# A one-element VectorE write ahead of GpSimd's first sum over the keys, in a band attention fused with a feed-forward layer

## The chip, the cores and the metric

The kernel runs on one core of one Trainium2 chip. The metric is the device time of one execution in microseconds (us); the time of a kernel is the median over its runs. Engines are named as the profile names them: PE is TensorE with its matmuls, PEld its weight loads, DVE is VectorE, ACT is ScalarE, POOL is GpSimd and SP is SyncE.

## The reference, cut to what matters

Attention over 8 batches of 8 heads, 576 positions and head size 64, in which each position sees itself and the 63 before it. Its output, as 4608 tokens of 512 numbers, goes through a feed-forward layer with 2048 hidden units.

```python
scores = scale * np.matmul(q, k.transpose(0, 1, 3, 2))
rel = pos[:, None] - pos[None, :]
scores = np.where((rel >= 0) & (rel < 64), scores, -1e9)
scores = scores - np.max(scores, axis=-1, keepdims=True)
attn = np.exp(scores)
attn = attn / (np.sum(attn, axis=-1, keepdims=True) + 1e-09)
x = np.matmul(attn, v).transpose(0, 2, 1, 3).reshape(4608, 512)
h = x @ w_in
out = np.maximum(0.01 * h, h) @ w_out
```

## The kernel before

**Attention.** The 576 positions of a batch are cut into nine blocks of 64 queries; each block of queries sees 128 keys. That makes 72 units, and two neighbouring units make a pair m. A pair's scores lie with the 128 keys on the partitions, in two halves j of 128x512 numbers. Maximum and sum over the keys are therefore taken across partitions, and POOL does both, with `partition_all_reduce`.

**Feed-forward.** The tokens are cut into nine chunks of 512, and the hidden units into sixteen blocks f of 128. One job (c, f) is 12 matmuls in `mm1` (line 539), which make 128 hidden units of 512 tokens, and 12 in `mm2` (line 586), which add their part of the output. Each product of two float32 tensors is made of three products of rounded parts: high by high, high by low, low by high. So after `mm1` ACT applies the leaky maximum (line 544, tile `g`) and rounds the result (line 550, tile `gh`), and then DVE subtracts to get the low part (line 554, tile `gl`). Four times in `mm2`, once for each 128 tokens, two matmuls with `gh` as weights are followed by one with `gl`. Tile `g` has one buffer, `gh` and `gl` have two each.

**The last stage.** The loop at the end of `band_attention_ffn` (from `open_room()` on) runs the jobs of chunks 2 to 8. Pairs 12 to 35 are worked in between them, two at a time: a group is eight jobs, numbered `at` from 0 to 7, with the pairs m (even, probabilities in tile `e`) and m + 1 (odd, in tile `late_e`). There are twelve groups; the last sixteen jobs have none. Below, "job 2 of a group" is the job with `at == 2`. Within a group:

- Job 1: after `mm1` and the `mm2` of job 0, PE makes the scores of both pairs (line 239); DVE scales and masks them (line 477); POOL takes the four maxima (line 486); DVE subtracts the maxima of pair m (line 492) and ACT takes the exponential (line 493). Then the `mm2` of job 1 is put in at once, so that the `mm1` of job 2 and of job 3 stand one behind the other on PE, followed by the `mm2` of job 2.
- Job 2: `mm1` with its leaky maximum, rounding and low part; then `exps_3(m + 1)`, the two subtractions of DVE and the two exponentials of ACT for the second pair; then three sums of POOL (line 497): pair m with j = 0 into slot 0 of tile `late_n`, pair m with j = 1 into the spare tile (`n` in the profile, tag `pT`), pair m + 1 with j = 0 into slot 1 of `late_n`.
- Job 4: `fold_3(m)` on DVE: two additions (lines 501 and 502) that bring the two halves' sums together, and a reciprocal (line 503). Then POOL's fourth sum, pair m + 1 with j = 1, into the spare tile that `fold_3(m)` has just read.
- Job 5: PE multiplies the probabilities of both pairs with the values (line 512); DVE does `product_3(m)`, `fold_3(m + 1)` and `low_3(m)`.
- Job 6: DVE does `product_3(m + 1)` and `low_3(m + 1)`.

The spare tile has one buffer. It holds the last maximum (pair m + 1, j = 1) until DVE has subtracted it, then the second sum, then the fourth. Slot 0 of `late_n` holds the maximum of pair m with j = 1 before it takes the first sum; slot 1 holds that of pair m + 1 with j = 0 before it takes the third.

**What sets the order.** The order on each engine is the order in which the program issues the instructions; a loop at the end of the function ties every instruction to the one before it on its engine. Between engines the framework adds waits from what each instruction reads and writes.

Of the kernel before, what the change touches and what calls it, by code (L numbers as in the profile page):

```python
# [88 lines left out]
def band_attention_ffn(ctx: ExitStack, tc: tile.TileContext, qT, kB, vW, vL, w_in, w_out, eye_mask, out):  # L89
    nc = tc.nc  # L90
# [49 lines left out]
    def load_q(m):  # L140
        if m < NU // 2:
            nc.sync.dma_start(q_of(m), qT[m])

    def load_k(m):
        if m < NU // 2:
            nc.sync.dma_start(k_of(m), kB[m])

    def load_v(m):
        if m < NU // 2:
            nc.sync.dma_start(v_of(m), vL[m - PAIRED] if m >= PAIRED else vW[m])  # L150
# [302 lines left out]
    later = {}  # L453
# [8 lines left out]
    def e_of(m):  # L462
        return (probs_of, later["e"])[m % 2]

    def scores_3(m):
        ps = [bank(t, f"s{m}_{j}") for j, t in enumerate((next(of_h), next(of_h)) if m % 2 else "st")]
        quarter_scores(m, ps, False)
        probs[m] = ps

    def shield_3(m):  # L470
        ps = probs.pop(m)
        a = mask_of(UNITS * m).bitcast(F32)
        n = a.shape[1]
        a = flat(a)[:, None, :].broadcast_to([P, H // n, n * QB])
        for j in range(2):
            e, s = (x.rearrange("a (b c) -> a b c", c=n * QB) for x in (e_of(m)[:, j], ps[j]))
            nc.vector.scalar_tensor_tensor(e, s, SCALE, a, ALU.mult, ALU.add)  # L477

    def spare(name):
        return wk.tile([P, 512], F32, tag="pT", bufs=1, name=name)  # L480

    def most_3(m):
        for j in range(2):
            b = 2 * (m % 2) + j
            mx = later["n"][:, b - 1] if b in (1, 2) else spare(f"mx{m}_{j}")
            nc.gpsimd.partition_all_reduce(mx, e_of(m)[:, j], P, ReduceOp.max)  # L486
            probs[m, j] = mx

    def exps_3(m):
        for j in range(2):  # L490
            e = e_of(m)[:, j]
            nc.vector.tensor_tensor(e, e, probs.pop((m, j)), ALU.subtract)  # L492
            nc.scalar.activation(e, e, AF.Exp)  # L493

    def sums_3(m, j):
        t = probs[m, "sum"] = spare(f"n{m}") if j else later["n"][:, m % 2]
        nc.gpsimd.partition_all_reduce(t, e_of(m)[:, j], P, ReduceOp.add)  # L497

    def fold_3(m):
        r, t = later["n"][:, m % 2], probs.pop((m, "sum"))  # L500
        nc.vector.tensor_scalar_add(r[64:], t[64:], 1e-9)  # L501
        nc.vector.tensor_scalar_add(r[:64], r[:64], 1e-9)
        nc.vector.reciprocal(r, r)  # L503

    def values_3(m):
        ps = bank("st"[m % 2], f"o{m}")
        for w in range(UNITS):
            v = v_heads(m, w)
            for p in range(NP):
                for j in range(2):  # L510
                    c = (2 * p + w) * QB
                    nc.tensor.matmul(  # L512
                        ps[64 * j : 64 * j + 64, c : c + QB], v[:, 2 * p + j], e_of(m)[:, j, c : c + QB],
                        start=True, stop=True,
                    )
        probs[m] = ps

    def product_3(m):
        r = later["n"][:, m % 2]
        nc.vector.tensor_tensor(r, probs.pop(m), r, ALU.mult)  # L520
        nc.scalar.copy(x_of(UNITS * m)[0], r.rearrange("a (b c) -> a b c", b=NP))

    def low_3(m):
        hi, lo = x_of(UNITS * m)
        t = later["n"][:, m % 2].rearrange("a (b c) -> a b c", b=NP)
        nc.vector.tensor_tensor(lo, t, hi.bitcast(F32), ALU.subtract)
# [5 lines left out]
    def mm1(c, f, part):  # L532

        xh, xl = xs[c]
        ps = bank(next(of_h) if c or f >= half else "h", f"h{c}_{f}_{part.start}")[:, part]
        wh, wl = wi[f]
        terms = [(a, b, k) for k in range(KT) for a, b in ((wh, xh), (wh, xl), (wl, xh))]
        for n, (a, b, k) in enumerate(terms):
            nc.tensor.matmul(ps, a[:, k, :], b[:, k, part], start=n == 0, stop=n == len(terms) - 1)  # L539
        t = []  # L540

        def leak():
            t.append(wk.tile([P, CH], F32, tag="g", bufs=1, name=f"g{c}_{f}_{part.start}")[:, part])
            nc.scalar.activation(t[0], ps, AF.Prelu, alpha=0.01)  # L544

        def high():
            g[c, f, part.start] = [
                wk.tile([P, CH], F32R, tag=n, name=f"{n}{c}_{f}_{part.start}") for n in ("gh", "gl")
            ]
            nc.scalar.copy(g[c, f, part.start][0][:, part], t[0])  # L550

        def low():
            hi, lo = (x[:, part] for x in g[c, f, part.start])
            nc.vector.tensor_tensor(lo, t[0], hi.bitcast(F32), ALU.subtract)  # L554

        return leak, high, low
# [13 lines left out]
    def mm2(c, f, part):  # L570


        gh, gl = g.pop((c, f, part.start))
        wh, wl = wo[f]
        for i in range(part.start // P, part.stop // P):
            split = c == 1 or c == 0 and i < 2
            begin = f == 0 or split and f == half
            end = f == FT - 1 or split and f == half - 1
            if begin:
                pool, tag = (ps_o, f"o{i}")  # L580
                if c == 1 and f == 0 and i > 1:
                    pool, tag = ps_e, "st"[i - 2]
                acc[c, i] = pool.tile([P, DM], F32, tag=tag, name=f"acc{c}_{i}_{f}")
            ts = slice(i * P, (i + 1) * P)
            for n, (a, b) in enumerate(((gh, wh), (gh, wl), (gl, wh))):
                nc.tensor.matmul(  # L586
                    acc[c, i], a[:, ts], b, start=begin and n == 0, stop=end and n == 2
                )
            if end:
                due.append(partial(evict, c, i, f, split))  # L590
# [24 lines left out]
    def flush():  # L615
        while due:
            due.pop(0)()
# [35 lines left out]
    def step(name):  # L653
        kind = name.rstrip("0123456789")
        return partial(acts[kind], int(name[len(kind) :]))
# [41 lines left out]
    for n, (c, f) in enumerate(steps):  # L697
        m = PAIRED + n // 8 * 2
        at = n % 8 if m < NU // 2 else None
        for step in mm1(c, f, whole):  # L700
            step()
        if at == 2:
            exps_3(m + 1)
            sums_3(m, 0)
            sums_3(m, 1)
            sums_3(m + 1, 0)
        if at == 4:
            fold_3(m)
            sums_3(m + 1, 1)
        if at == 5:  # L710
            for x in (m, m + 1):
                values_3(x)
                load_v(x + 2)
            product_3(m)
            fold_3(m + 1)
            low_3(m)
        if at == 6:
            product_3(m + 1)
            low_3(m + 1)
        if prev:  # L720
            mm2(*prev)
            flush()
        prev = (c, f, whole)
        if at == 1:
            for x in (m, m + 1):
                scores_3(x)
                load_q(x + 2)
            load_k(m + 2)
            load_k(m + 3)
            shield_3(m)  # L730
            shield_3(m + 1)
            most_3(m)
            exps_3(m)
            most_3(m + 1)
            mm2(*prev)
            flush()
            prev = None
# [61 lines left out]
```

## Time and profile before

| | |
|---|---|
| median of 3 runs | 916.51 us (916.43 to 916.56) |
| profiled execution, its own time | 916.39 us |
| its span in the profile, first to last instruction | 914.6 us |
| granted TensorE clock | 1.000 of full speed |
| DVE busy | 501.5 us (55%) |
| ACT busy | 304.7 us (33%) |
| POOL busy | 315.4 us (34%) |

A row of the timeline gives the start of an instruction, its duration, both in us, its engine, its line, its operation, the tile that it writes and those that it reads; in brackets stands how long the engine had been idle before it, and which instruction ended that. "x12" says that twelve neighbours were put into one row. Matmuls overlap one another, so the pace of PE is the distance between starts and not the duration of a row: a row of 12 matmuls that lasts 2.88 us is followed by the next one's start sooner than that.

The first group's scores are made at 239.5 us of the span and its four maxima begin at 241.57; the last group's maxima begin at 784.53.

### The profile page before, as it was taken

The page shows a single profiled execution, that of the slowest core. Times are in us where ns is not written, and L with a number is a line of the kernel's source. Part 1 is how long each engine was busy: PE and PEld are TensorE (multiplying, and loading weights), DVE is VectorE, ACT ScalarE, POOL GpSimd, SP SyncE. Part 2 cuts the span into 40 slices and gives each one's busy share as a digit, 9 for nine tenths or more (in the row PEclk, how much of TensorE's full clock was granted, in tenths as well). Part 3 has the DMA queues.
Part 4 walks back from the last instruction along what each step waited for, and adds up shares of the span by engine and source line. Part 5 has one row for each costly group of instructions (what it writes and reads, how often), then busy time and mean ns, then how long its engine had stood idle before and what let it go on. Part 6 is the DMA issues. An engine that isn't in the chain of part 4 may idle for free.

```text
span 914.6 us, 16196 instructions
## 1 busy us (share of the span) xinstructions
PE 894.1 (98%) x7021; PEld 731.6 (80%) x7021; DVE 501.5 (55%) x638; ACT 304.7 (33%) x517; POOL 315.4 (34%) x132
## 2 busy tenths in 40 slices
PE   8999999999999999999999999999999999999998
PEld 5887888888788787878787878878787878788886
DVE  7999991587563736264554646373726365461111
ACT  4665662233232233233322232222323322223222
POOL 4431000673442617080716244351708070620000
PEclk9999999999999999999999999999999999999999
DMA  8753641233211121012211121112101211001001
GB/s 290 261 171 121 223 136 70 71 135 110 93 47 47 47 70 62 8 47 73 67 47 47 47 94 47 47 48 85 52 3 47 91 49 47 2 1 47 0 1 47
DMA packets 30359, 68.48 MB, mean 75 GB/s; under 512 B 3024, under 2 KB 3152, under 8 KB 30288
## 3 DMA queue, kind: packets, MB, share of 16 engines
q1 hardware_dynamic: 25824, 51.75, 16.3%
q10 hardware_dynamic: 4464, 15.70, 5.5%
q8 instruction: 55, 0.90, 0.4%
q14 instruction: 16, 0.13, 0.0%
HBM read 56.43 MB, written 11.01 MB: 74 GB/s over the span
## 4 chain that ended last, share of the span: by engine, by line
PE 79%; DVE 13%; ACT 3%; POOL 3%; issue 1%; DMA 1%; ACTq 0%; DVEq 0%
PE acc L586 38%; PE h L539 34%; DVE gl L554 4%; PE o L512 3%; POOL late_n L486 2%; PE s L239 2%; DVE e L492 2%; DVE e L477 2%; DVE late_e L477 2%; ACT e L493 1%; ACT gh L550 1%; ACT g L544 1%; PE o L328 1%; DVE raw L202 1%; DMA room<-eye_mask 1%
## 5 line engine op out<-in xcount | busy, mean ns | idle before, releaser
L539 PE MATMUL h<-x,wi 128*128 128x512 f32 (+1 forms) x1440 | 336.8, 384 | 0.1
L554 DVE TENSOR_TENSOR gl<-g,gh 128x512 fp32r<-128x512 f32 (+1 forms) x147 | 132.5, 902 | 350.0 <-ACT gh L550 349.8
L539 PEld LDWEIGHTS h<-x,wi 128*128 128x128 f32 x1440 | 265.7, 188 | 54.3 <-DVE x L362 0.4
L586 PE MATMUL acc<-wo,gh 128*128 128x512 f32 x936 | 293.0, 394 | 0.3 <-DVE s L603 0.3
L586 PEld LDWEIGHTS acc<-wo,gh 128*128 128x128 f32 x936 | 172.8, 188 | 37.0 <-DVE s L603 0.5
L544 ACT ACTIVATE g<-h 128x512 f32<-128x512 f32 (+1 forms) x147 | 86.4, 588 | 338.8 <-PE h L539 337.5
L586 PE MATMUL acc<-wo,gl 128*128 128x512 f32 x468 | 184.0, 393 | 12.5 <-DVE gl L554 12.5
L486 POOL PARTITION_ALL_REDUCE mx<-e x12 | 21.4, 1782 | 331.1 <-DVE e L477 331.1
L586 PEld LDWEIGHTS acc<-wo,gl 128*128 128x128 f32 x468 | 87.8, 188 | 35.8 <-DVE gl L554 17.6
L550 ACT CAST gh<-g 128x512 fp32r<-128x512 f32 (+1 forms) x147 | 90.0, 612 | 9.3 <-PE acc L586 4.4
L503 DVE RECIPROCAL late_n<-late_n 128x512 f32<-128x512 f32 x24 | 80.5, 3353 | 0.8
L539 PE MATMUL h<-x,w 128*128 128x512 f32 x324 | 77.8, 389 | 0.0
L539 PEld LDWEIGHTS h<-x,w 128*128 128x128 f32 x324 | 60.8, 188 | 12.6
L586 PE MATMUL acc<-w,gh 128*128 128x512 f32 x216 | 66.7, 390 | 0.0
L393 POOL PARTITION_ALL_REDUCE mx<-e x8 | 15.2, 1900 | 94.1 <-DVE e L385 90.8
L586 PEld LDWEIGHTS acc<-w,gh 128*128 128x128 f32 x216 | 40.5, 188 | 8.5
L493 ACT ACTIVATE e<-e 128x512 f32<-128x512 f32 x24 | 15.2, 632 | 95.2 <-DVE e L492 95.2
L497 POOL PARTITION_ALL_REDUCE n<-e x12 | 38.8, 3234 | 11.1 <-ACT late_e L493 11.1
L497 POOL PARTITION_ALL_REDUCE n<-late_e x12 | 40.5, 3377 | 5.3 <-DVE late_n L501 5.3
L586 PE MATMUL acc<-w,gl 128*128 128x512 f32 x108 | 42.0, 389 | 0.0
L497 POOL PARTITION_ALL_REDUCE late_n<-e x12 | 39.8, 3313 | 0.0
L497 POOL PARTITION_ALL_REDUCE late_n<-late_e x12 | 39.7, 3311 | 0.0
(98 smaller groups left out, 793.1 us busy)
## 6 DMA issues: line engine op xcount, KB each, us to landing
q<-qT SPq DMA_DIRECT2D x34, 256.0 KB, 3.3
raw<-w_out ACTq DMA_DIRECT2D x15, 512.0 KB, 3.7
out<-o SPq DMA_DIRECT2D x30, 256.0 KB, 2.1
raw<-w_in ACTq DMA_DIRECT2D x14, 512.0 KB, 3.7
k<-kB SPq DMA_DIRECT2D x25, 256.0 KB, 3.5
v<-vL SPq DMA_DIRECT2D x12, 512.0 KB, 3.8
late_v<-vL SPq DMA_DIRECT2D x12, 512.0 KB, 4.2
v<-vW SPq DMA_DIRECT2D x8, 520.0 KB, 5.4
```

Of the source, the lines that this page charges most:

```text
L239: nc.tensor.matmul(ps[j][t, c : c + QB], k[i][s, p], q[s, w, p], start=not begun and (not more or (w, p) == (0, 0)), stop=not begun and no ...
L477: nc.vector.scalar_tensor_tensor(e, s, SCALE, a, ALU.mult, ALU.add)
L486: nc.gpsimd.partition_all_reduce(mx, e_of(m)[:, j], P, ReduceOp.max)
L493: nc.scalar.activation(e, e, AF.Exp)
L497: nc.gpsimd.partition_all_reduce(t, e_of(m)[:, j], P, ReduceOp.add)
L503: nc.vector.reciprocal(r, r)
L512: nc.tensor.matmul(ps[64 * j : 64 * j + 64, c : c + QB], v[:, 2 * p + j], e_of(m)[:, j, c : c + QB], start=True, stop=True,)
L539: nc.tensor.matmul(ps, a[:, k, :], b[:, k, part], start=n == 0, stop=n == len(terms) - 1)
L544: nc.scalar.activation(t[0], ps, AF.Prelu, alpha=0.01)
L550: nc.scalar.copy(g[c, f, part.start][0][:, part], t[0])
L554: nc.vector.tensor_tensor(lo, t[0], hi.bitcast(F32), ALU.subtract)
L586: nc.tensor.matmul(acc[c, i], a[:, ts], b, start=begin and n == 0, stop=end and n == 2)
```

## The change

One DVE instruction is put into each group at job 2, between `exps_3(m + 1)` and the first sum. It writes a zero into one element of slot 0 of `late_n`, on one partition.

```diff
         if at == 2:
             exps_3(m + 1)
+
+            nc.vector.memset(later["n"][:1, 0, :1], 0.0)
             sums_3(m, 0)
             sums_3(m, 1)
             sums_3(m + 1, 0)
```

The first sum writes the whole of slot 0, that element too, so the written zero never reaches the result. But the framework sees two writes to one place and lets POOL's first sum wait for DVE's write. DVE works in order, and ahead of this write stand the low part of job 2 and the two subtractions of pair m + 1. Nothing else is moved, and no transfer is touched.

## Prediction

> **What bounds the kernel now.** I read the page's head first, to see which engine has no time left.
>
> ```profile
> span 914.6 us, 16196 instructions
> PE 894.1 (98%) x7021; PEld 731.6 (80%) x7021; DVE 501.5 (55%) x638; ACT 304.7 (33%) x517; POOL 315.4 (34%) x132
> ```
>
> PE is busy for 894.1 of 914.6 us; DVE, ACT and POOL have about half their time or more to spare. So a change on DVE and POOL can matter only where PE waits for them. The next view is therefore the waits of PE alone, from 240 to 800 us of the span, where the groups lie:
>
> ```profile
> PE acc L586 <- DVE gl L554: 12.5, 12, 1.0
> ```
>
> It is the only wait that this view lists: twelve times, once a group, about 1.0 us, and each time for DVE's low part. The timeline of PE in the first group shows the place, and the last group's shows that it is the same there:
>
> ```profile
> 249.82 0.61 PE L586 MATMUL acc<-wo,gh 128*128 128x512 f32 x2
> 251.48 0.50 PE L586 MATMUL acc<-wo,gl 128*128 128x512 f32 x1 [1.04 <-DVE gl L554]
> ...
> 253.88 2.88 PE L539 MATMUL h<-x,wi 128*128 128x512 f32 x12
> 256.60 0.61 PE L586 MATMUL acc<-wo,gh 128*128 128x512 f32 x2
> ...
> 259.32 2.88 PE L539 MATMUL h<-x,wi 128*128 128x512 f32 x12
> ...
> 270.17 0.39 PE L586 MATMUL acc<-wo,gl 128*128 128x512 f32 x1
> ```
>
> ```profile
> 792.78 0.61 PE L586 MATMUL acc<-wo,gh 128*128 128x512 f32 x2
> 794.44 0.50 PE L586 MATMUL acc<-wo,gl 128*128 128x512 f32 x1 [1.04 <-DVE gl L554]
> ...
> 796.86 2.88 PE L539 MATMUL h<-x,wi 128*128 128x512 f32 x12
> ```
>
> The `mm2` of job 2 starts at 249.82, does two matmuls with `gh`, and then stands until `gl` is there. Undisturbed, twelve matmuls take 2.72 us from start to start (256.60 to 259.32, the `mm2` of job 3), 0.227 each. The disturbed `mm2` takes 253.88 - 249.82 = 4.06 us in the first group and 796.86 - 792.78 = 4.08 in the last. So the stall costs 4.07 - 2.72 = 1.35 us a group. That is more than the 1.04 of the wait's row, because a matmul's row outlasts its place in the pipeline: the third matmul was due at 249.82 + 2 x 0.227 = 250.27 and came at 251.48, 1.21 late, and the other 0.14 is lost in the restart (a row of 0.50 where the others have 0.39).
>
> Why is `gl` late? POOL and DVE side by side in the same group:
>
> ```profile
> 243.26 1.86 POOL L486 PARTITION_ALL_REDUCE late_n<-e  x1
> 245.03 1.86 POOL L486 PARTITION_ALL_REDUCE late_n<-late_e  x1
> 246.79 1.86 POOL L486 PARTITION_ALL_REDUCE mx<-late_e  x1
> 248.56 3.31 POOL L497 PARTITION_ALL_REDUCE late_n<-e  x1
> 252.80 3.23 POOL L497 PARTITION_ALL_REDUCE n<-e  x1 [0.93 <-ACT late_e L493]
> 255.94 3.31 POOL L497 PARTITION_ALL_REDUCE late_n<-late_e  x1
> 259.69 3.38 POOL L497 PARTITION_ALL_REDUCE n<-late_e  x1 [0.45 <-DVE late_n L501]
> ```
>
> ```profile
> 243.39 1.53 DVE L492 TENSOR_TENSOR e<-e,mx 128x512 f32<-128x512 f32 x1 [0.19 <-POOL mx L486]
> 245.16 1.53 DVE L492 TENSOR_TENSOR e<-e,late_n 128x512 f32<-128x512 f32 x1 [0.23 <-POOL late_n L486]
> 248.65 2.77 DVE L554 TENSOR_TENSOR gl<-g,gh 128x512 fp32r<-128x512 f32 x1 [1.96 <-ACT gh L550]
> 251.35 0.68 DVE L492 TENSOR_TENSOR late_e<-late_e,late_n 128x512 f32<-128x512 f32 x1
> 251.95 0.68 DVE L492 TENSOR_TENSOR late_e<-late_e,mx 128x512 f32<-128x512 f32 x1
> 254.47 1.12 DVE L554 TENSOR_TENSOR gl<-g,gh 128x512 fp32r<-128x512 f32 x1 [1.84 <-ACT gh L550]
> 258.08 0.72 DVE L554 TENSOR_TENSOR gl<-g,gh 128x512 fp32r<-128x512 f32 x1 [2.49 <-ACT gh L550]
> 258.83 0.69 DVE L501 TENSOR_SCALAR late_n<-n 64x512 f32<-64x512 f32 x1
> 259.55 0.42 DVE L502 TENSOR_SCALAR late_n<-late_n 64x512 f32<-64x512 f32 x1
> 260.01 3.35 DVE L503 RECIPROCAL late_n<-late_n 128x512 f32<-128x512 f32 x1
> 263.51 0.69 DVE L554 TENSOR_TENSOR gl<-g,gh 128x512 fp32r<-128x512 f32 x1 [0.16 <-ACT gh L550]
> 264.12 0.68 DVE L520 TENSOR_TENSOR late_n<-o,late_n 128x512 f32<-128x512 f32 x1
> 264.84 0.42 DVE L501 TENSOR_SCALAR late_n<-n 64x512 f32<-64x512 f32 x1
> ```
>
> The low part takes 0.69 to 0.72 us where POOL is idle or two thirds through a sum (263.51, 258.08). At 248.65 it starts 0.09 behind the first sum and takes 2.77. It ends at 251.42, 2.86 after the sum's start. At 254.47 it starts in the middle of the second sum, takes 1.12 and ends 2.79 after that sum's start; the subtraction at 243.39 ends 1.66 after the start of its maximum. So a DVE instruction with two inputs in SBUF that meets a POOL reduction doesn't end before 2.8 us into a sum, or 1.66 into a maximum, whenever it started. I call this the hold. The reciprocal, with one input, takes its 3.35 us right behind the fourth sum's start (259.69), so it isn't held. The chain is then: POOL's first sum starts because its maxima are done, 0.09 us before the low part is ready; it holds the low part for 2.08 us (2.77 - 0.69); PE loses 1.35 of them.
>
> **The change part by part.** *The low part of job 2.* The first sum now starts behind it. What else could hold it is the last maximum, from 246.79; its hold ends 1.66 later, at 248.45, before 248.65. So `gl` runs from 248.65 to 249.34, 0.93 us ahead of PE's third matmul at 250.27. The stall goes: 12 x 1.35 = 16.2 us, if nothing else comes late.
>
> *The written element itself.* One write more on DVE, and the two subtractions ahead of it. The write's price is nowhere in this trace; the nearest row is the zeroing of a whole 128x512 tile near the start:
>
> ```profile
> L647 DVE MEMSET wi<- x1: 485/485/485, 0.9 to 0.9; 128x512 f32 x1
> ```
>
> So it lies between 0 and 0.49 us; a gain is excluded, as an added instruction in order can't shorten DVE's queue. I take 0.1, near the lower end, for one element in place of 65,536. On PE's path it costs nothing at either end: behind it on DVE stands the low part of job 3, which is not ready for another 1.7 us (below).
>
> *The sums move back.* The subtractions end 1.21 us after the low part (252.63 against 251.42), now at 250.55; the write at 250.65; from a release to POOL's start it takes 0.17 (252.63 to 252.80). The first sum starts at 250.82 instead of 248.56. The spare tile, for which the second sum waited until now, is free by then, so the three sums run back to back, each starting 0.09 before the other's row ends (252.80 + 3.23 against 255.94): at 250.82, 254.04 and 257.18. The second and third are 1.24 later than before while PE is 1.35 earlier. Who waits for that?
>
> *The low part of job 3.* ACT's rows say when it is ready:
>
> ```profile
> 252.06 1.23 ACT L493 ACTIVATE late_e<-late_e 128x512 f32<-128x512 f32 x2 [3.45 <-DVE late_e L492]
> 253.20 0.58 ACT L544 ACTIVATE g<-h 128x512 f32<-128x512 f32 x1
> 253.81 0.62 ACT L550 CAST gh<-g 128x512 fp32r<-128x512 f32 x1
> ```
>
> The two exponentials stand ahead of the leaky maximum of job 3, and they follow the first subtraction, which comes 2.08 us earlier. All three rows move with it, and the low part is ready at 254.47 - 2.08 = 252.39. That falls into the first sum, so it is held until 250.82 + 2.86 = 253.68. PE needs it as the third matmul of job 3's `mm2`: 256.60 - 1.35 + 0.45 = 255.70. It has 2.0 us to spare, and with the dearest write still 1.6.
>
> *The fold of pair m.* The low part of job 4 moves with PE from 258.08 to 256.73 and ends at 257.42, or at 260.04 if the third sum (257.18) holds it; PE wants it after the values' product, at 270.17 - 5.44 - 1.35 = 263.38 (one job is 24 matmuls, 5.44 us). Line 501 took 0.69 inside the third sum and 0.42 without POOL (264.84), and ended 3.58 after that sum's start. If it is held as long now, it ends at 257.18 + 3.58 = 260.76, 1.24 later than before. The fourth sum and the reciprocal follow at the old distances: 260.93, and 261.25 to 264.60. Queued behind the reciprocal is the low part of job 5, then at 265.3 instead of 264.2. PE wants it at 270.17 - 1.35 = 268.82, so 3.5 us are left. Behind it follow the product 0.68, line 501 0.42, line 502 0.42, the reciprocal 3.35 and one low part of x and one of job 6 at about 0.7 each: 271.6, against a need at 268.82 + 5.44 = 274.26. Each cover holds by 2 us or more. No transfer is moved.
>
> The sum: the profiled execution took 916.39 us (span 914.6), 0.12 below the median of 916.51. 916.39 - 16.2 = **900.2 us**.
>
> Here one rule of the Trainium skill speaks against the change. "SBUF — State Buffer", section "Who interferes with whom", says that whichever of GpSimd and VectorE issues first has the shared ports for its whole instruction, while the other blocks fully. The trace agrees that the later one waits and disagrees on how long: the low part ended at 251.42, when the sum's row still had 0.45 us to go (248.56 + 3.31 = 251.87). What a strict rule would do to the low part of job 3 is the second rival.
>
> **The rivals.** *Only what the wait's row counts comes back.* If the restart and the overlap of the rows cost PE nothing, the gain is 12.5 us: 916.39 - 12.5 = 903.9. Against it stands the distance of the starts, 4.06 against 2.72 for the same twelve matmuls.
>
> *The hold passes from sum to sum.* Now three sums stand back to back, where 0.93 us lay between the first and the second. If the low part of job 3, waiting since 252.39, doesn't get in while the first sum runs out, it meets the second and is free at 254.04 + 2.79 = 256.83. Against the need at 255.70, with 0.06 us to PE's start and 0.14 for the restart, that is 1.33 us a group: 916.39 - 16.2 + 12 x 1.33 = 916.2, no change. If it doesn't get in before the third either, it is free at 260.04: 4.54 us a group, 916.39 - 16.2 + 54.5 = 954.7, slower. It decides at 255.70: an end before that costs nothing. Against both: the subtractions at 243.39 and 245.16 each ended while POOL went through maxima back to back, and the low part at 254.47 ended at 255.59, 0.35 before the third sum that followed the second without a gap. For it: none of them had waited from the first sum of a row of sums. By the page's rule, a wait until the sum's whole row is over (250.82 + 3.31 = 254.13, after the next sum's start at 254.04) would lead here.
>
> *The wait isn't there.* If one element doesn't order the two writes, the first sum starts at 248.56 as now, and the write costs at most 12 x 0.49 us on a DVE that has room behind it: 916.4. Against it: the sum writes the same element, and the waits come from such overlaps.
>
> **How the numbers follow.** 900.2 is the likeliest, with a chance of 0.82; the wait's row alone 0.06; the hold passing once 0.04, and twice 0.04; no wait 0.04. What a measurement of this kernel can tell from no change is about 0.2%, 1.8 us. Faster by more than that: 0.82 + 0.06 = 0.88; within it: 0.04 + 0.04 = 0.08; slower: 0.04. The forecast's own bounds: 12 x 1.21 = 14.5 if the restart's loss stays (901.9), and 0.5 below 900.2 for the scatter of the runs and the rounding of twelve differences (899.7). These hold about 0.75; the range reaches up to the first rival, so that 2 in 10 at most are left out: 899.7 to 904.0.
>
> **What would show it.** PE's waits no longer list the low part, or under 0.1 us a time; the `mm2` of job 2 takes 2.72 us from start to start; the low part of job 2 is 0.69 long and that of job 3 about 1.3, held by the first sum; the first sum starts some 2.2 us after the last maximum's end, and three sums stand without a gap; a new row for the write, of some 0.1 us; the distance from group to group falls by 1.35 us. The prediction is wrong if the low part of job 3 ends after the second sum's start, if the first sum still starts on the heels of the maxima, or if PE waits at a new place.

## The result and the profile after

The kernel with the change takes 900.8 us in the median (900.04 to 901.43, four runs) against 916.47 us for the kernel before (916.41 to 916.56): a ratio of 0.9829, with a 95% interval from 0.9812 to 0.9846. The prediction was 900.2 us.

The profiled execution took 901.12 us, with a span of 899.3. The view of PE's waits from 240 to 800 us, which listed one row before, has only its two head lines left:

```profile
core 0 of [0], span 899.3 us
engine line waited for: us in total, times, longest us
```

PE in the first group: the `mm2` of job 2 now takes 253.44 - 250.72 = 2.72 us from start to start (4.06 before), and its first matmul with `gl` follows 0.45 us after the start.

```profile
250.72 0.62 PE L586 MATMUL acc<-wo,gh 128*128 128x512 f32 x2
251.17 0.39 PE L586 MATMUL acc<-wo,gl 128*128 128x512 f32 x1
...
253.44 2.88 PE L539 MATMUL h<-x,wi 128*128 128x512 f32 x12
256.16 0.62 PE L586 MATMUL acc<-wo,gh 128*128 128x512 f32 x2
256.61 0.39 PE L586 MATMUL acc<-wo,gl 128*128 128x512 f32 x1
```

The last two rows are the `mm2` of job 3, whose low part PE wants at 256.61.

POOL's sums and DVE beside them, in the same group:

```profile
251.66 3.23 POOL L497 PARTITION_ALL_REDUCE late_n<-e  x1 [2.11 <-ACT late_e L493]
254.79 3.31 POOL L497 PARTITION_ALL_REDUCE n<-e  x1
258.01 3.42 POOL L497 PARTITION_ALL_REDUCE late_n<-late_e  x1
261.33 3.46 POOL L497 PARTITION_ALL_REDUCE n<-late_e  x1
```

```profile
249.54 0.69 DVE L554 TENSOR_TENSOR gl<-g,gh 128x512 fp32r<-128x512 f32 x1 [1.96 <-ACT gh L550]
250.15 0.68 DVE L492 TENSOR_TENSOR late_e<-late_e,late_n 128x512 f32<-128x512 f32 x1
250.75 0.68 DVE L492 TENSOR_TENSOR late_e<-late_e,mx 128x512 f32<-128x512 f32 x1
251.38 0.06 DVE L705 MEMSET late_n<- 1x1 f32 x1
253.27 1.17 DVE L554 TENSOR_TENSOR gl<-g,gh 128x512 fp32r<-128x512 f32 x1 [1.83 <-ACT gh L550]
257.64 0.69 DVE L554 TENSOR_TENSOR gl<-g,gh 128x512 fp32r<-128x512 f32 x1 [3.20 <-ACT gh L550]
258.36 2.35 DVE L501 TENSOR_SCALAR late_n<-n 64x512 f32<-64x512 f32 x1
260.75 0.95 DVE L502 TENSOR_SCALAR late_n<-late_n 64x512 f32<-64x512 f32 x1
261.73 3.35 DVE L503 RECIPROCAL late_n<-late_n 128x512 f32<-128x512 f32 x1
```

The low part of job 2 takes 0.69 us, the write 0.06, and the first sum starts 0.22 us after the write's end. All four sums stand without a gap. (The bracket behind the first sum names ACT's exponentials of the second pair, which that sum neither reads nor overwrites; releasers are inferred, and what it has to wait for is DVE's write, which the bracket names in variant 5 below, `[4.63 <-DVE late_n L705]`.)

From the first group's maxima to the last's it is now 770.6 - 242.47 = 528.1 us for eleven distances, 48.01 each, against 49.36 before: 1.35 us a group, the predicted figure. Twelve of them are 16.2 us. The spans differ by 914.6 - 899.3 = 15.3, because in this execution the first maxima came 0.9 us later (242.47 against 241.57), in the stage ahead of the groups, which the change does not touch.

Was the hold taken away, or only moved? The groups of DVE rows by line answer that. Before:

```profile
L554 DVE TENSOR_TENSOR gl<-g,gh 128x512 fp32r<-128x512 f32 (+1 forms) x147 | 132.5, 902 | 350.0 <-ACT gh L550 349.8
...
L501 DVE TENSOR_SCALAR late_n<-n 64x512 f32<-64x512 f32 x24 | 13.4, 558 | 0.8
...
L502 DVE TENSOR_SCALAR late_n<-late_n 64x512 f32<-64x512 f32 x24 | 10.1, 419 | 0.5
```

After:

```profile
L554 DVE TENSOR_TENSOR gl<-g,gh 128x512 fp32r<-128x512 f32 (+1 forms) x147 | 107.0, 728 | 334.8 <-ACT gh L550 334.6
...
L501 DVE TENSOR_SCALAR late_n<-n 64x512 f32<-64x512 f32 x24 | 33.3, 1389 | 0.7
...
L502 DVE TENSOR_SCALAR late_n<-late_n 64x512 f32<-64x512 f32 x24 | 16.5, 687 | 0.5
```

The low parts lost 25.5 us of busy time, and lines 501 and 502 gained 26.3. DVE as a whole is as busy as before (500.8 us against 501.5). So the hold has moved from an instruction that PE waits for to two that it does not wait for.

### The profile page after: what moved, and what is told of

Same layout as the page of the kernel before. It is cut to its first block, busy times and chain, and to the rows that moved or that the text cites. A ratio compares the mean times of both kernels' runs of the same rounds, so it can differ in the third digit from the quotient of the medians.

```text
span 899.3 us, 16208 instructions
## 1 busy us (share of the span) xinstructions
PE 888.7 (99%) x7021; PEld 731.0 (81%) x7021; DVE 500.8 (56%) x650; ACT 304.5 (34%) x517; POOL 316.4 (35%) x132
## 4 chain that ended last, share of the span: by engine, by line
PE 93%; DVE 5%; DMA 1%; ACT 0%; issue 0%; ACTq 0%
PE acc L586 43%; PE h L539 42%; PE s L239 4%; PE o L512 3%; DVE raw L190 1%; DVE raw L202 1%; DVE raw L194 1%; DVE w L207 1%; DMA room<-eye_mask 1%; PE o L328 1%; PE o L424 0%; DVE gl L554 0%; DVE wi L214 0%; DVE y L347 0%; DVE e L298 0%
## 5 line engine op out<-in xcount | busy, mean ns | idle before, releaser
L554 DVE TENSOR_TENSOR gl<-g,gh 128x512 fp32r<-128x512 f32 (+1 forms) x147 | 107.0, 728 | 334.8 <-ACT gh L550 334.6
```

## The experiments

The theory: the first sum, already at work, holds up the low part of job 2, because that reads two inputs from SBUF, and PE loses 1.35 us a group by it; any way to keep the two apart brings the same time, and what is late instead costs nothing as long as it lies within its slack. The rivals: the written element or the place of the code matters; the subtractions and exponentials of the second pair matter and not the low part; the cause is the order of the sums and not the second SBUF input. "Distance" is the mean time from one group's first maximum to the next one's, in the profiled execution. Each row is measured beside the kernel before on the same chip. Variants 1, 2, 4, 9, 10 and 11 are edits of the kernel before; the edits shown under 3, 5 and 7 are against the kernel with the change, and 6 goes one step further than 5.

| | us, median | ratio to before (95% interval) | distance, us |
|---|---|---|---|
| before | 916.46 to 916.72 | 1 | 49.36 |
| 1: write into slot 1 | 916.6 | 1.0001 (0.9992 to 1.0011) | 49.37 |
| 2: first two sums exchanged | 900.31 | 0.9825 (0.981 to 0.984) | 48.01 |
| 3: wait for the low part alone | 904.09 | 0.9866 (0.9852 to 0.9881) | 48.30 |
| 4: no first sum | 900.36 | 0.9824 (0.9809 to 0.9839) | 48.01 |
| 5: sums behind job 3 | 900.21 | 0.9823 (0.9809 to 0.9838) | 48.01 |
| 6: sums behind job 4 | 947.44 | 1.0341 (1.0325 to 1.0356) | 52.05, of two kinds |
| 7: write of the whole slot | 900.46 | 0.9827 (0.9812 to 0.9841) | 48.01 |
| 8: the change again | 900.25 | 0.9826 (0.981 to 0.9843) | 48.01 |
| 9: sums exchanged, fold as before | 900.56 | 0.9821 (0.9806 to 0.9836) | 48.01 |
| 10: low part of job 2 from PSUM | 900.92 | 0.9824 (0.9808 to 0.984) | 48.01 |
| 11: low parts of jobs 2 and 3 from PSUM | 901.09, one run | 0.982 beside one run of 917.28 | 48.01 |

**1. The write without the wait.**

```diff
             exps_3(m + 1)
+            nc.vector.memset(later["n"][:1, 1, :1], 0.0)
             sums_3(m, 0)
```

> The one-element write stays, in the same place of DVE's queue, but goes into slot 1 of the tile, where it orders the third sum and not the first. Theory (the first sum's hold on the low part of job 2 costs PE 1.35 us a group, and only the order of those two matters): the first sum again starts on the heels of the maxima, the low part of job 2 takes 2.77 us, the mm2 of job 2 takes 4.07 us from start to start: 916.5 us. Rival (an added DVE instruction, or where the code comes to lie, makes the gain, and the order of the sums does not): about 900.8 us as with the change.

The time is that of the kernel before. The first sum starts on the heels of the maxima again and the low part of job 2, 0.09 us behind it, is held. The write (0.06 us) is there, behind that low part and both subtractions in DVE's queue, but the first sum does not wait for it:

```profile
249.11 3.31 POOL L497 PARTITION_ALL_REDUCE late_n<-e  x1
```

```profile
249.20 2.77 DVE L554 TENSOR_TENSOR gl<-g,gh 128x512 fp32r<-128x512 f32 x1 [1.96 <-ACT gh L550]
```

So neither the instruction nor the place of the code brings the gain; the wait does.

**2 and 9. The wait without the write.**

```diff
-            sums_3(m, 0)
             sums_3(m, 1)
+            sums_3(m, 0)
```

> No write. The first two sums of pair m change places: the sum with j = 1 goes first, and it has to wait anyway until DVE has read the last maximum out of the spare tile, which is behind the low part of job 2 and both subtractions. Theory: the same order of low part and sums as with the change, so the same gain without an added instruction: 900.8 us, between 900.0 and 901.5; the first sum starts 0.17 us after the second subtraction, the low part of job 2 takes 0.69 us. Rival (the write itself does something): 916.5 us.

The program remembers the tile of the sum issued last, so in this variant the fold takes both halves' sums from slot 0, and the fourth sum does not wait for the fold; its output is not that of the reference. Variant 9 has the same exchange and keeps the fold's operands:

```diff
-        t = probs[m, "sum"] = spare(f"n{m}") if j else later["n"][:, m % 2]
+        t = spare(f"n{m}") if j else later["n"][:, m % 2]
+        if j:
+            probs[m, "sum"] = t
```

> No write. The sum of pair m with j = 1 goes first and has to wait for the spare tile, as in the earlier exchange of the two sums; here the fold still takes the second half's sum from the spare tile, so that the fourth sum again waits for the fold's first addition. Theory: 900.3 us, between 900.0 and 901.2, the same as the change within 0.1%, with the same instructions as the kernel before. Rival (the fourth sum's wait or the missing write moves a need): 902 us or more, or a PE wait for the low part.

Both come out as the theory has it. POOL and DVE in variant 9 (its added lines shift the numbers by two, so the low part is line 556):

```profile
251.00 3.23 POOL L499 PARTITION_ALL_REDUCE n<-e  x1 [2.06 <-ACT late_e L493]
```

```profile
248.94 0.69 DVE L556 TENSOR_TENSOR gl<-g,gh 128x512 fp32r<-128x512 f32 x1 [1.96 <-ACT gh L552]
...
250.15 0.68 DVE L492 TENSOR_TENSOR late_e<-late_e,mx 128x512 f32<-128x512 f32 x1
```

The sum starts 0.17 us after the second subtraction (250.15 + 0.68 = 250.83). No instruction is added, and the time cannot be told from that of the change.

**4. The first sum left out.**

```diff
-            sums_3(m, 0)
             sums_3(m, 1)
```

> The kernel before without POOL's first sum in each group (pair m, j = 0); it leaves that sum out, and the fold takes in its place what stands in slot 0. No write is added. Theory: with nothing of POOL beside it the low part of job 2 takes 0.69 us, PE's stall is gone, and the time is that of the change: 900.8 us, between 900.0 and 901.5. Rival (PE's stall has another cause that the change removes as well, for instance the exponentials ahead of ACT's work for job 3): the stall stays and the time is between 905 and 916 us.

The variant leaves a sum out, so its output is not that of the reference; it is there for its time. The low part of job 2 is free:

```profile
249.05 0.69 DVE L554 TENSOR_TENSOR gl<-g,gh 128x512 fp32r<-128x512 f32 x1 [1.96 <-ACT gh L550]
```

The gain is there in full, 0.9824, in the old order and without any write. The first sum's being there at that moment was the whole cost.

**3. Only the low part goes ahead.**

```diff
+            nc.vector.memset(later["n"][:1, 0, :1], 0.0)
             exps_3(m + 1)
-            nc.vector.memset(later["n"][:1, 0, :1], 0.0)
             sums_3(m, 0)
```

> The write stands ahead of the two subtractions of the second pair, directly behind the low part of job 2, so that the first sum waits for the low part alone and runs beside the subtractions. Theory (a held DVE instruction costs time only if PE needs what it or its followers make): the low part of job 2 is free (0.69 us) and its 1.35 us come back, but the second subtraction is now held until some 2.8 us into the first sum, the exponentials of the second pair and behind them on ACT the leaky maximum of job 3 come about 2.5 us later than with the change, and the low part of job 3 falls into the second sum: it ends near or after the need of mm2 of job 3. From no new wait to one of 0.5 us a group: 900.8 to 907 us. Rival (the gain comes from the subtractions and exponentials being early, not from the low part of job 2): most of the gain is lost, 912 us or more.

Three quarters of the gain remain. DVE and PE in the first group:

```profile
250.09 0.69 DVE L554 TENSOR_TENSOR gl<-g,gh 128x512 fp32r<-128x512 f32 x1 [1.96 <-ACT gh L550]
250.71 0.69 DVE L492 TENSOR_TENSOR late_e<-late_e,late_n 128x512 f32<-128x512 f32 x1
250.72 0.06 DVE L703 MEMSET late_n<- 1x1 f32 x1
251.31 2.73 DVE L492 TENSOR_TENSOR late_e<-late_e,mx 128x512 f32<-128x512 f32 x1
255.88 1.38 DVE L554 TENSOR_TENSOR gl<-g,gh 128x512 fp32r<-128x512 f32 x1 [1.84 <-ACT gh L550]
```

```profile
256.70 0.61 PE L586 MATMUL acc<-wo,gh 128*128 128x512 f32 x2
257.31 0.50 PE L586 MATMUL acc<-wo,gl 128*128 128x512 f32 x1
```

The low part of job 2 is free, and now the second subtraction is held (2.73). Behind it the exponentials and job 3's work on ACT come late, and job 3's low part ends at 257.26, where its matmul was due at 256.70 + 0.45 = 257.15. It came at 257.31 and restarts with a row of 0.50, so PE loses 0.16 and the restart: the distance is 0.29 us longer than with the change, 3.5 us in all. The view of PE's waits does not list this one, since the row before it covers the gap. So with the low part of job 2 free its `mm2` takes 253.98 - 251.26 = 2.72 us and the 1.35 us are back, but 0.29 of them are lost again at job 3. The write has to stand behind the subtractions too, to keep those 0.29.

**7. A dearer write.**

```diff
-            nc.vector.memset(later["n"][:1, 0, :1], 0.0)
+            nc.vector.memset(later["n"][:, 0], 0.0)
```

> As the change, but the write covers the whole of slot 0, 128x512 in place of one element, 0.49 us in place of 0.06. Theory (the write is off PE's path by the 2.0 us that the low part of job 3 has to spare): the sums start 0.4 us later, the low part of job 3 ends 0.4 later, and the time stays: 900.8 us, between 900.0 and 901.5. Rival (what stands in DVE's queue there counts in full): 0.43 x 12 = 5.2 us more, 906 us.

The write takes 0.48 us, the low part of job 3 takes 1.66 in place of 1.17, and the time stays.

**5 and 6. How late may the sums be?** The write and the three sums go one job later, then two (in variant 6 right ahead of the first fold). The edit of variant 5:

```diff
         if at == 2:
             exps_3(m + 1)
+        if at == 3:
             nc.vector.memset(later["n"][:1, 0, :1], 0.0)
             sums_3(m, 0)
```

> As the change, but write and first three sums stand one job later, behind the low part of job 3, which is then not held at all; everything of POOL comes about 2.6 us later than with the change. Theory (the sums have slack, and a late sum costs only when the low part of job 5, queued behind the reciprocal of the first fold, misses its mm2): that low part ends at about 268.3 against a need at 269.7, the one of job 6 at about 274.4 against 275.2: no wait of PE, 900.8 us, between 900.0 and 901.5. Rival (the distance at which the sums run matters by itself, or the slack was misjudged): PE waits at job 5 or 6, 905 us or more. Times are those of the first group in the profile of the change.

> As the change, but write and sums stand two jobs later, behind the low part of job 4 and right ahead of the first fold. Theory: the fold waits for the second sum until about 265.1, its first addition is held by the third sum, its reciprocal ends near 272.1, and the low part of job 5, queued behind it, is ready at about 272.7 where PE wants it at 269.7: a wait of about 3.0 us, then a smaller one of about 0.5 at job 6. About 3.2 to 3.8 us a group, 940 to 946 us: slower than the kernel before. Rival (a later sum costs nothing, since POOL has time left): 900.8 us.

In variant 5 the first sum starts 4.63 us after the last maximum's end, and PE waits for nothing: 900.21 us. In variant 6 it is 9.00 us, and PE waits for the low part of job 5, as the expectation had it:

```profile
269.20 0.61 PE L586 MATMUL acc<-wo,gh 128*128 128x512 f32 x2
272.40 0.50 PE L586 MATMUL acc<-wo,gl 128*128 128x512 f32 x1 [2.59 <-DVE gl L554]
...
275.65 3.67 PE L539 MATMUL h<-x,wi 128*128 128x512 f32 x12
279.16 0.62 PE L586 MATMUL acc<-wo,gh 128*128 128x512 f32 x2
```

The mean cost is 52.05 - 48.01 = 4.04 us a group, above the expected 3.2 to 3.8, but the groups are of two kinds: six distances are about 52.5 us and five about 51.5, that is 4.5 and 3.5 more than with the change. In the first kind PE is slower after the gap. In the first group the twelve matmuls from 275.65 take 3.51 us from start to start in place of 2.72, and the windows of that stretch show the granted clock at 0.76 of full speed from 272 to 279 us, and at 1.00 before and after (columns: length, busy time of PE, PEld, DVE, ACT and POOL with their instructions, granted clock, DMA share, GB/s):

```profile
240.00:272.00 32.00, 29.81 (x304) 24.40 (x302) 15.81 (x16) 7.26 (x12) 20.11 (x8) 1.00 0.21 67
272.00:279.00 7.00, 6.60 (x22) 5.27 (x23) 6.88 (x8) 1.74 (x4) 0.00 (x0) 0.76 0.01 2
279.00:291.00 12.00, 12.00 (x55) 9.92 (x54) 2.08 (x3) 3.68 (x7) 0.00 (x0) 1.00 0.00 0
```

The same 7 us are at 0.76 in six of the twelve groups and at 1.00 in the other six, behind a wait of the same length (2.58 to 2.59 us). In those other six the second, smaller wait that was expected at job 6 appears, of 0.23 to 0.28 us. So the expectation had the loss by the waits right, and what it lacked is about 1 us of slower clock in every second group. What decides which groups get it was not tried.

**8. The scatter.**

> The change itself, unaltered, on the chip on which its variants run, and once more profiled. Theory: 900.8 us; the scatter of 1.4 us between its executions comes from the stage before the first group, so its groups again follow one another at 48.01 us and a difference in the span equals the difference in where the first group's maxima start (242.47 in the first profile). Rival (the groups themselves vary): the distance between groups differs from 48.01.

The distance is 48.01 us again. In the profiled execution, of 900.24 us, the first maxima came at 241.6 and the span was 898.5: 0.9 us earlier and 0.8 us shorter than in the first profile. So this difference lies in the stage ahead of the groups. What makes that stage vary was not tried.

**10 and 11. Is it the second SBUF input?** The order of the kernel before, but the result of the leaky maximum goes back into the PSUM bank that `mm1` has written, and not into tile `g` in SBUF: in variant 10 for job 2 (`at == 2` in the last row), in variant 11 for jobs 2 and 3:

```diff
-    def mm1(c, f, part):
+    def mm1(c, f, part, keep=False):
...
-            t.append(wk.tile([P, CH], F32, tag="g", bufs=1, name=f"g{c}_{f}_{part.start}")[:, part])
+            t.append(ps if keep else wk.tile([P, CH], F32, tag="g", bufs=1, name=f"g{c}_{f}_{part.start}")[:, part])
...
-        for step in mm1(c, f, whole):
+        for step in mm1(c, f, whole, at in (2, 3)):
```

> The order of the kernel before, no write; but in job 2 of each group ACT writes the leaky result back into its PSUM bank instead of into tile g, so that the low part of that job reads one input from PSUM and one from SBUF. Theory (what the first sum holds up is DVE's second SBUF input): the first sum starts on the heels of the maxima as before, yet the low part of job 2 beside it takes about 0.7 us in place of 2.77, PE's stall is gone, and the two subtractions take the hold instead, to 2.86 us into the first sum; the low part of job 3 then falls early into the second sum and still ends about 0.5 us ahead of its need: 900.3 us, between 900.0 and 902.5. Rival (POOL's sums hold up any DVE instruction, or the stall comes from the order alone): the low part of job 2 again takes 2.8 us and the time is 916 us.

> As the variant whose low part of job 2 reads PSUM, but job 3 as well. There the low part of job 2 came 0.03 us ahead of the first sum, so it did not show what a sum already at work does to it; the low part of job 3, from tile g, started 1.67 us into the second sum and took 1.12. Theory (only a second SBUF input is held): the low part of job 3 starts at the same place in the second sum and takes about 0.69 us. Rival (any DVE instruction that starts inside a sum is held to 2.8 us from the sum's start): 1.1 us again. Time 900.3 us, between 900.0 and 902.5, for both.

Variant 10 has the full gain, but ACT was quicker too, and the low part of job 2 came just ahead of the sum (249.76 against 249.79), so that it alone could not tell the kind of input from who comes first. Variant 11 can. Its POOL and DVE rows, from the first sum on:

```profile
249.42 3.31 POOL L497 PARTITION_ALL_REDUCE late_n<-e  x1
253.05 3.23 POOL L497 PARTITION_ALL_REDUCE n<-e  x1 [0.32 <-ACT late_e L493]
```

```profile
249.40 0.69 DVE L554 TENSOR_TENSOR gl<-h,gh 128x512 fp32r<-128x512 f32 x1 [1.85 <-ACT gh L550]
250.01 2.28 DVE L492 TENSOR_TENSOR late_e<-late_e,late_n 128x512 f32<-128x512 f32 x1
252.21 0.68 DVE L492 TENSOR_TENSOR late_e<-late_e,mx 128x512 f32<-128x512 f32 x1
254.69 0.69 DVE L554 TENSOR_TENSOR gl<-h,gh 128x512 fp32r<-128x512 f32 x1 [1.80 <-ACT gh L550]
```

The low part of job 3 starts 1.64 us into the second sum and takes 0.69, as all 24 low parts of this form do; from tile `g` it took 1.12 at that place. The subtraction at 250.01, with two inputs in SBUF, is held in the same trace to 252.29, 2.87 us into the first sum. The rival that any DVE instruction is held falls. In its section "Who interferes with whom", the Trainium skill's "SBUF — State Buffer" says the same of the kind of input: an instruction of VectorE with at most one SBUF input, outside its two-port modes, does not contend with GpSimd. The trace agrees, with 0.69 us. The number of inputs is not the whole rule, though: the last section has additions with one input that are held.

## Why the prediction was right

*The stall and its size.* The step that mattered was to read 1.35 us a group from the distance of PE's starts and not 1.04 from the wait's row. The distance of the groups fell by 49.36 - 48.01 = 1.35. The first rival, 903.9 us from the row alone, lies outside all four runs.

*The low part of job 2.* 0.69 us, as predicted. Variants 1 and 4 show from both sides that the first sum beside it was the cause: the write without the wait gives nothing, no sum gives everything.

*The write.* Taken at 0.1 us between 0 and 0.49; it is 0.06, and variant 7 shows that 0.48 costs nothing either.

*The sums and the low part of job 3.* The first sum was to start 1.48 us after the low part of job 2 (250.82 against 249.34); it was 1.43 (251.66 against 250.23). The low part of job 3 was to end 2.86 us into the first sum, 2.0 us ahead of its need; it ended 2.78 us into it, at 254.44, against 256.61. So the hold did not pass on to the second sum. In variant 5 the low part of job 4 met the second of three sums without a gap; POOL's and DVE's rows there:

```profile
256.42 3.31 POOL L497 PARTITION_ALL_REDUCE n<-e  x1
259.64 3.31 POOL L497 PARTITION_ALL_REDUCE late_n<-late_e  x1
```

```profile
256.74 2.55 DVE L554 TENSOR_TENSOR gl<-g,gh 128x512 fp32r<-128x512 f32 x1 [3.67 <-ACT gh L550]
```

It started 0.32 us into that sum and ended 2.87 into it, at 259.29, before the third started. So there as well the hold was not passed on.

*The fold of pair m: mis-sized, without effect.* Line 501 was to end 3.58 us into the third sum, and the fourth sum to follow it. In the trace line 501 ended 2.70 into that sum (258.36 + 2.35 = 260.71) and line 502, which was not expected to be held, took 0.95 in place of 0.42. The reciprocal started 0.4 us earlier than predicted (261.73; 261.25 and the 0.9 of the later start are 262.15), and the fourth sum, at 261.33, did not have to wait. Variant 5 took more out of this slack and still cost nothing; variant 6 took all of it and cost 947.44 - 900.21 = 47.2 us against variant 5.

*The total.* 900.2 was the sum for one execution whose first stage takes 241.57 us. The four runs lie from 900.04 to 901.43, and the variants that remove the same stall have medians of 900.21 to 900.92.

## What to carry to other kernels

When two engines share something, look for the instruction that the bounding engine waits for and ask what is at work beside it when it starts; a wait that costs the other engine some microseconds can be free, if what it delays has slack. Read the size of a stall from the distance between starts, against the same stretch without it, and not from the wait's row. And before adding an instruction for the sake of a wait, see whether an order exists in which another operand enforces it: exchanging two sums did the same here.

## What the runs showed that was not expected

- One-input additions are held too. Line 501 took 2.35 us and line 502 0.95 beside the third sum, against 0.42 without one, while the reciprocal right behind them took its 3.35 inside the fourth sum. Line 501 ended 2.70 us into the sum and line 502 3.69, so the first got in while the sum was still at work. That a sum holds DVE in two stretches, with a gap between them, would fit; no run measured it by itself.
- The hold has a price on POOL's side as well. With nothing of DVE ahead of it, a sum after a pause of POOL took 3.23 us and one right behind another POOL instruction 3.31. Where DVE's subtraction came 0.29 us ahead of a sum after a pause (variant 3), the sum took 3.49; where the low part came 0.37 ahead of the third sum, right behind the second (the change), that took 3.42. With an operand in PSUM and 0.03 us ahead of a sum right behind the maxima (variant 10) it took 3.31.
- A gap of 2.75 us on PE (272.40 against 269.65, variant 6) was followed by 7 us at a mean granted clock of 0.76 in six of the twelve groups, and by a clock of 1.00 in the other six. So a gap of this length can cost clock and need not. Behind the gaps of 1.21 us in the kernel before nothing of the kind shows, its clock is 1.000.
